# Transposing DMA of f by rows of four tokens (2 KB), with a sigmoid that puts the tokens back in order

## The chip, the cores and the metric

One core of a Trainium2 chip; the batches of runs fell on different chips, and every ratio is taken within a batch. The metric is the time of one execution in device microseconds (us). A run is called fast or slow: slow when it is more than 1.5% above the fastest run of the same kernel. Only fast runs are compared.

Engines: PE is TensorE (matmuls), PEld its weight loads, ACT is ScalarE, DVE is VectorE, POOL is GpSimd, SP is SyncE, whose queue (SPq) issues most DMAs here.

## The reference

A gated recurrence over 6,144 tokens of 4 sequences, 256 wide, feeds a two-layer feed-forward block:

```python
sig = 1.0 / (1.0 + np.exp(-f_logit))
f = lower_bound + (1.0 - lower_bound) * sig
h = f[:, t] * h + (1.0 - f[:, t]) * x[:, t]        # y[:, t] = h, over all t
h1, h2 = y @ w1, y @ w2                            # 256 -> 1024
out = np.maximum(h1, h2) @ w_out                   # 1024 -> 256
```

The kernel computes max(h1, h2) as h1 + relu(h2 - h1), so the first layer is one product with wd = w2 - w1, and h1 goes into the second layer through a precomputed 256 x 256 matrix. With u = sigmoid(-f_logit) the decay is 1 - (1 - lower_bound) u and the drive u x; the factor 1 - lower_bound is folded into the weights.

## The kernel before

The work goes in 48 blocks of 512 tokens. The recurrence needs the tokens along the free dimension and d on the partitions. The first 2,048 tokens are turned on TensorE; from then on (22 chunks of 1,024 tokens, 44 blocks) a GpSimd DMA casts f and x to bf16 into a DRAM scratch, and a transposing DMA on the SP queue brings them into SBUF turned:

```python
    def cross(c):
        nt = chunks[c][2]
        for s in range(2):                      # s = 0 is f, s = 1 is x
            if by_xbar(c, s):
                dst = inpool.tile([P, KC, CH], BF16, name=("fT", "xT")[s])
                nc.sync.dma_start_transpose(
                    out=dst[:, :, 0:nt], in_=held[c, s][0:nt, :]
                )
                held[c, s] = dst
```

The sigmoid of a block, and VectorE's five steps after it:

```python
    def gate(j):
        nb = blocks[j][2]
        u = midpool.tile([P, KC, TB], BF16, name="u")
        fT = turned[j, 0]
        nc.scalar.activation(
            out=like(u[:, :, 0:nb], fT), in_=fT, func=AF.Sigmoid, scale=-1.0
        )
        us[j] = u
    # scan_steps(j): decay(0), decay(1), drive (u * x), scan(0), scan(1)  -> y
```

The first layer of a block writes eight PSUM tiles dT, which ScalarE evicts with a relu, in the same queue as the sigmoids:

```python
    def first_layer(j, fc):
        # ... two matmuls of 512 columns into dT (pool ps_d, 3 buffers)
        nc.scalar.activation(out=rt[:, 0:nb], in_=dT[:, 0:nb], func=AF.Relu)
```

The main loop interleaves, for each of eight slots of block j, one first_layer of j and an eighth of the second layer of j - 1 (five matmuls of 256 columns), and puts the sigmoid of block j + 1 behind the eviction of slot 0:

```python
            for fc in range(FC):
                if j < NBLK:
                    first_layer(j, fc)
                if j > 2:
                    second_layer(j - 1, fc)
                # ... (turns on TensorE, first blocks only)
                if fc in gates:
                    gate(gates[fc])             # slot 0 for transposed chunks
                if fc == 0 and 2 < j < NBLK - 1:
                    scans = scan_steps(j + 1)
                if fc < len(scans):
                    scans[fc]()
```

## Time and profile before

| | before |
|---|---|
| timed runs | 400.79 us median of 3 (400.66 to 400.88) |
| profiled execution | 430.05 us, span 428.3 us, state slow |

The profile page, with the span, each engine's busy time, then TensorE and its granted clock in 40 slices of the span (busy tenths), then the chain of work that ended last:

```profile
span 428.3 us, 6970 instructions
...
PE 392.8 (92%) x2744; PEld 296.8 (69%) x2792; DVE 248.7 (58%) x359; ACT 268.5 (63%) x447; POOL 26.4 (6%) x58
...
PE   3999979798789999998997899999998999999996
...
PEclk9999999999989999999999699999999999999999
...
PE 46%; DMA 34%; SPq 15%; ACT 3%; DVE 1%; issue 1%; ACTq 0%
```

TensorE has holes between the sixth slice and the thirty-first, and a third of the chain is DMA. The windows of the same trace show two neighbouring blocks where nothing disturbs it, and one stretch where something does. The columns are the stretch, its length, then busy time and instructions of PE, PEld, DVE, ACT and POOL, the granted clock, the DMA share and GB/s:

```profile
323.63:331.45 7.82, 7.77 (x55) 5.96 (x56) 5.29 (x8) 5.50 (x10) 0.00 (x0) 1.00 1.21 195
331.45:339.27 7.82, 7.77 (x55) 5.95 (x56) 4.73 (x8) 5.49 (x9) 0.97 (x2) 1.00 1.02 220
110.00:120.00 10.00, 5.97 (x41) 4.26 (x40) 2.41 (x6) 4.01 (x8) 0.72 (x2) 0.98 0.99 152
```

A block takes 7.82 us when TensorE is fed. The instructions on the tile fT, the transposed f (duration min/median/max), and the DMAs' time from issue to landing:

```profile
L190 ACT ACTIVATE u<-fT x44: 1048/1051/1146, 41.2 to 405.5; 128x1024 bf16<-128x1024 bf16 x44
...
DMA to landing us min/median/max: 7.2/15.8/22.4
```

The sigmoid takes 1.05 us; f takes 15.8 us to land in this execution. A second look at the same kernel (b0_look), taken after the prediction, caught the fast state: it is a single run, to which the record gives no state, but at 400.91 us and a granted clock of 0.999 it lies with the fast ones. It is the one to compare with. Page, then the instructions on fT:

```profile
span 399.0 us, 7018 instructions
...
PE 388.5 (97%) x2792; PEld 295.0 (74%) x2792; DVE 249.1 (62%) x359; ACT 269.7 (68%) x447; POOL 26.3 (7%) x58
...
PE   3999999999999999999999999999999999999996
...
PE 97%; DMA 2%; SPq 1%; issue 0%; DVE 0%
```

### The profile page before, as it was taken

To read this page: it belongs to the slowest core of one execution; us is meant where nothing else is said; L and a number is where in the kernel's file an instruction comes from. 1 tells how busy PE (TensorE), PEld (TensorE's weight loads), DVE (VectorE), ACT (ScalarE), POOL (GpSimd) and SP (SyncE) were. 2 spreads that over 40 slices of the span, in tenths; PEclk is the share of its full clock that TensorE was granted. 3 is DMA by queue.
4 is the path that set the end of the run, shared out by engine and by line. 5 is a ranking of instruction groups with operands and counts; after the bars stand their busy time and mean duration, and the time that the engine had idled before them with its cause. 6 is when DMAs were issued, how large, how long until landed. Compare 5 with 4: busy or idle time off the path is not lost.

```text
span 428.3 us, 6970 instructions
## 1 busy us (share of the span) xinstructions
PE 392.8 (92%) x2744; PEld 296.8 (69%) x2792; DVE 248.7 (58%) x359; ACT 268.5 (63%) x447; POOL 26.4 (6%) x58
## 2 busy tenths in 40 slices
PE   3999979798789999998997899999998999999996
PEld 1677756576557777776775577767676777777775
DVE  5785637455357566564653557657547656567551
ACT  3656656557366676675673666756657676776762
POOL 1400000000000000000000000000000000000000
PEclk9999999999989999999999699999999999999999
DMA  7999999999999999999998999999999999998112
GB/s 245 222 220 198 123 157 141 137 169 252 81 240 226 119 239 233 112 248 168 183 237 75 218 158 186 250 145 170 219 131 231 226 216 164 268 157 179 79 69 100
DMA packets 103377, 77.01 MB, mean 180 GB/s; under 512 B 93552, under 2 KB 94064, under 8 KB 102640
## 3 DMA queue, kind: packets, MB, share of 16 engines
q1 hardware_dynamic: 100512, 51.13, 66.7%
q0 software_dynamic: 2544, 25.17, 36.1%
q8 instruction: 22, 0.36, 0.4%
q10 hardware_dynamic: 288, 0.26, 0.2%
q14 instruction: 11, 0.09, 0.1%
HBM read 53.48 MB, written 48.23 MB: 237 GB/s over the span
## 4 chain that ended last, share of the span: by engine, by line
PE 46%; DMA 34%; SPq 15%; ACT 3%; DVE 1%; issue 1%; ACTq 0%
PE psO L410 25%; DMA fT<-scr_0_90 20%; PE dT L381 19%; SPq L153 13%; DMA fT<-scr_1_91 12%; ACT u L190 2%; DMA w1n_110<-in_moe_w_dram 2%; SPq L433 1%; PE psO L352 1%; ACT rt L389 1%; PE tT L180 1%; PE psO L365 0%; SPq L121 0%; DVE osb L430 0%; DVE y L233 0%
## 5 line engine op out<-in xcount | busy, mean ns | idle before, releaser
L389 ACT ACTIVATE rt<-dT 128x512 bf16<-128x512 f32 x384 | 219.2, 598 | 104.1 <-PE dT L381 100.0
L381 PE MATMUL dT<-y,wd 128*128 128x512 bf16 x720 | 219.5, 384 | 21.3 <-ACT rt L389 19.5
L410 PE MATMUL psO<-wob,rt 128*128 128x256 bf16 x1536 | 230.7, 274 | 2.7 <-issue 0.4
L410 PEld LDWEIGHTS <-rt 128*128 128x128 bf16 x1536 | 170.7, 114 | 41.4 <-issue 1.1
L233 DVE TENSOR_TENSOR_SCAN y<-ff,y,v 128x512 bf16<-128x512 bf16 x88 | 107.9, 1268 | 0.1
L430 DVE COPY osb<-psO 128x512 f32<-128x512 f32 x94 | 64.7, 690 | 59.0 <-PE psO L410 58.9
L381 PEld LDWEIGHTS <-wd 128*128 128x128 bf16 x768 | 75.8, 99 | 33.2 <-issue 24.6
L209 DVE TENSOR_SCALAR ff<-u,nom 128x512 bf16<-128x512 bf16 x94 | 29.0, 351 | 105.0 <-ACT u L190 105.0
L410 PE MATMUL psO<-w_109,y 128*128 128x256 bf16 x384 | 74.0, 275 | 0.0
L410 PEld LDWEIGHTS <-y 128*128 128x128 bf16 x384 | 43.4, 113 | 42.6 <-issue 3.5
L190 ACT ACTIVATE u<-fT 128x1024 bf16<-128x1024 bf16 x44 | 46.4, 1054 | 35.5 <-DMA fT<-scr_1_91 18.2
L220 DVE TENSOR_TENSOR v<-u,xT 128x1024 bf16<-128x1024 bf16 x44 | 30.3, 688 | 3.8 <-DMA xT<-scr_0_92 1.8
L98 POOL DMA_DIRECT2D scr_0_90<-in_f_logit_dram x11 | 5.4, 493 | 149.7 <-DMA fT<-scr_0_90 149.7
L98 POOL DMA_DIRECT2D scr_1_91<-in_f_logit_dram x11 | 5.3, 486 | 148.8 <-DMA fT<-scr_1_91 148.1
L233 DVE TENSOR_TENSOR_SCAN y<-ff,v 128x512 bf16<-128x512 bf16 x6 | 7.0, 1208 | 0.0
L98 POOL DMA_DIRECT2D scr_0_92<-in_x_dram x11 | 5.4, 488 | 18.7 <-DMA xT<-scr_0_92 16.9
L98 POOL DMA_DIRECT2D scr_1_93<-in_x_dram x11 | 5.3, 486 | 15.7 <-DMA xT<-scr_1_93 14.9
L190 ACT ACTIVATE u<-tT 128x1024 bf16<-128x1024 bf16 x3 | 3.2, 1058 | 4.3 <-PE tT L180 4.3
L352 PE MATMUL psO<-ident_f,w1n_110 128*128 128x128 f32 x8 | 1.9, 422 | 3.4 <-DMA w1n_110<-in_moe_w_dram 3.4
L341 ACT ACTIVATE wd<-wdf,om 128x128 bf16<-128x128 f32 (+1 forms) x6 | 2.2, 428 | 4.3 <-DVE wdf L333 4.3
L352 PEld LDWEIGHTS psO<-ident_f,w1n_110 128*128 128x128 f32 x8 | 1.6, 221 | 3.7 <-issue 3.7
L220 DVE TENSOR_TENSOR v<-u,tT 128x1024 bf16<-128x1024 bf16 x3 | 3.6, 1216 | 0.0
(49 smaller groups left out, 45.1 us busy)
## 6 DMA issues: line engine op xcount, KB each, us to landing
out_dram<-osb SPq DMA_DIRECT2D x47, 512.0 KB, 4.8
scr_0_90<-in_f_logit_dram POOLq DMA_DIRECT2D x11, 512.0 KB, 7.5
scr_0_92<-in_x_dram POOLq DMA_DIRECT2D x11, 512.0 KB, 12.4
scr_1_91<-in_f_logit_dram POOLq DMA_DIRECT2D x11, 512.0 KB, 7.9
scr_1_93<-in_x_dram POOLq DMA_DIRECT2D x11, 512.0 KB, 13.6
fn<-in_f_logit_dram POOLq DMA_DIRECT2D x3, 256.0 KB, 7.9
xn<-in_x_dram POOLq DMA_DIRECT2D x3, 256.0 KB, 8.6
w2n_112<-in_moe_w_dram SPq DMA_DIRECT2D x1, 512.0 KB, 6.5
```

The lines of the kernel that those rows point to most:

```text
L98: nc.gpsimd.dma_start(out=scr[0:nt, :].rearrange("(p i) d -> p (i d)", p=P), in_=src.rearrange("(p i) d -> p (i d)", p=P),)
L153: nc.sync.dma_start_transpose(out=dst[:, :, 0:nt], in_=held[c, s][0:nt, :])
L180: nc.tensor.transpose(dst, src, ident[:])
L190: nc.scalar.activation(out=like(u[:, :, 0:nb], fT), in_=fT, func=AF.Sigmoid, scale=-1.0)
L209: nc.vector.tensor_scalar(out=ff[:, h, 0:nb], in0=u[:, h, 0:nb], scalar1=nom[:, h : h + 1], scalar2=1.0, op0=ALU.mult, op1=ALU.add,)
L220: nc.vector.tensor_tensor(out=like(v[:, :, 0:nb], xT), in0=like(u[:, :, 0:nb], xT), in1=xT, op=ALU.mult,)
L233: nc.vector.tensor_tensor_scan(out=y[:, h, 0:nb], data0=ff[:, h, 0:nb], data1=v[:, h, 0:nb], initial=init, op0=ALU.mult, op1=ALU.add,)
L352: nc.tensor.transpose(pt[:, kc, q, :], half(w1n, g)[:, kc, 2 * r + q], ident_f[:])
L381: nc.tensor.matmul(dT[:, 0:nb], lhsT=wd[:, kc, fc * P : (fc + 1) * P], rhs=y[:, kc, 0:nb], start=(kc == 0), stop=(kc == KC - 1),)
L389: nc.scalar.activation(out=rt[:, 0:nb], in_=dT[:, 0:nb], func=AF.Relu)
L410: nc.tensor.matmul(ps[:, r, :], lhsT=left, rhs=right, start=(s == 0 and (r == 0 or j == NBLK - 1)), stop=(s == n - 1 and (r == 1 or j == N ...
L430: nc.vector.tensor_copy(out=osb[:, 2 * g : 2 * g + 2, :], in_=ps[:])
```

## The change

The intent: the transposing DMA of f should read long rows. The 1,024 x 256 scratch is seen as 256 rows of 4 tokens (2 KB) in place of 1,024 rows of one (512 B). The result has f sorted by the position i of the token in its row: all tokens 0, 4, 8, ..., then 1, 5, 9, .... The sigmoid has to pass over all of f anyway, so it puts the tokens back: it reads runs of one i (128 neighbouring elements) and writes u with a step of 4 elements. x stays as it was, so that VectorE's multiply keeps its contiguous operands.

```diff
@@ cross
+                if wide_rows[s]:                      # (True, False): f only; RT = 4
+                    dst = inpool.tile([P, RT, KC, CH // RT], BF16, name=("fT", "xT")[s])
+                    nc.sync.dma_start_transpose(
+                        out=dst[:].rearrange("p i k r -> p (i k) r"),
+                        in_=held[c, s][0:nt, :].rearrange("(r i) d -> r (i d)", i=RT),
+                    )
+                    held[c, s] = dst[:].rearrange("p i k r -> p k r i")
+                else:
                     # ... as before
@@ gate
-        nc.scalar.activation(
-            out=like(u[:, :, 0:nb], fT), in_=fT, func=AF.Sigmoid, scale=-1.0
-        )
+        out = like(u[:, :, 0:nb], fT)
+        if by_xbar(blocks[j][3], 0):
+            out, fT = by_row(out), by_row(fT)
+        nc.scalar.activation(out=out, in_=fT, func=AF.Sigmoid, scale=-1.0)
@@
+    def by_row(t):
+        return t if len(t.shape) == 3 else t.rearrange("p k m i -> p k i m")
```

More of the change, by code (lines that the diff above doesn't have):

```diff
@@ L80 @@
     NSCR = 2
+    RT = 4
+    wide_rows = (True, False)
     scratch = [
@@ L151, in cross @@
             if by_xbar(c, s):
-                dst = inpool.tile([P, KC, CH], BF16, name=("fT", "xT")[s])
-                nc.sync.dma_start_transpose(
-                    out=dst[:, :, 0:nt], in_=held[c, s][0:nt, :]
-                )
-                held[c, s] = dst
+                if wide_rows[s]:
[6 more added lines that the diff above has]
+                else:
+                    dst = inpool.tile([P, KC, CH], BF16, name=("fT", "xT")[s])
+                    nc.sync.dma_start_transpose(
+                        out=dst[:, :, 0:nt], in_=held[c, s][0:nt, :]
+                    )
+                    held[c, s] = dst
     def turn_steps(j):
@@ L162, in turn_steps @@
             if by_xbar(c, s):
-                turned[j, s] = held[c, s][:, :, o : o + nb]
+                if wide_rows[s]:
+                    turned[j, s] = held[c, s][:, :, o // RT : (o + nb) // RT, :]
+                else:
+                    turned[j, s] = held[c, s][:, :, o : o + nb]
                 continue
@@ L189, in gate @@
         fT = turned[j, 0]
-        nc.scalar.activation(
-            out=like(u[:, :, 0:nb], fT), in_=fT, func=AF.Sigmoid, scale=-1.0
-        )
+        out = like(u[:, :, 0:nb], fT)
+        if by_xbar(blocks[j][3], 0):
+            out, fT = by_row(out), by_row(fT)
+        nc.scalar.activation(out=out, in_=fT, func=AF.Sigmoid, scale=-1.0)
         us[j] = u
@@ L197, in like @@
             return t
-        return t.rearrange("p k (m i) -> p k m i", m=P)
+        return t.rearrange("p k (m i) -> p k m i", m=src.shape[2])
+    def by_row(t):
+        return t if len(t.shape) == 3 else t.rearrange("p k m i -> p k i m")
     def scan_steps(j):
@@ L219, in drive @@
             xT = turned[j, 1]
+            operands = [like(v[:, :, 0:nb], xT), like(u[:, :, 0:nb], xT), xT]
+            if by_xbar(c, 1):
+                operands = [by_row(t) for t in operands]
             nc.vector.tensor_tensor(
-                out=like(v[:, :, 0:nb], xT),
-                in0=like(u[:, :, 0:nb], xT),
-                in1=xT,
-                op=ALU.mult,
+                out=operands[0], in0=operands[1], in1=operands[2], op=ALU.mult
             )
```

## The prediction

> **What bounds it now.** TensorE. From 323.6 to 339.3 us the windows show it busy 7.77 of every 7.82 us, one 512-token block each. Before about 32 us come block 0, the weights and block 1's first layer; after it 47 second and 46 first layers, 46.7 block times, about 365 us; then 4 us of tail. That sums to 401 us, plus 1.8 us between the profiled span (428.3) and its measured time (430.05). The timed runs take 400.79, so by this estimate they hardly stall. The profiled execution is 27 us longer: the windows show about 22 us of TensorE holes between 50 and 330 us, and the granted clock (mean 0.986, 0.78 at 230 us) explains about 6. The holes are waits for f: the chain of waits has 32% in f's transposes and 13% in the SP queue's issue of transposes. I take them for a property of the profiled execution, which must also record 103,377 DMA packets. On that reading the prediction hangs.
>
> **Why f is late there.** An f transpose takes a median 15.8 us from issue to landing, x's 9.3. The packet records show all 90,112 transposing packets at 256 B, median 18 ns, mean 35: 677 of them take over 1.28 us and make up 77 of 198 us per engine. They stand behind the casting DRAM-to-DRAM loads, whose 32 KB pieces take 2.5 us or more on the same engines. Undisturbed, x's transpose moves in 2.0 to 2.5 us (128 packets an engine at 18 ns). f's time is mostly company, not row length.
>
> **What the change does.** 22 transposes read 256 rows of 2 KB in place of 1,024 of 512 B. Bytes, loads, buffers, waits and instruction counts stay. The Trainium skill, "DMA: Bandwidth & Descriptors", section "SDMA does more than copy", gives the crossbar transpose as one of 256-byte tiles; this trace agrees (256 B packets although rows are 512 B). So I expect still 2,048 packets of 256 B per transpose, near 18 ns, and f's landing still set by the loads beside it. If the longer rows made longer packets, f would save at most 1 to 2 of its 2.3 us per chunk of 15.6 us of TensorE work. The danger is the opposite: 256 B read at a pitch of 2 KB might be slower.
>
> The sigmoid (44, mean 1,054 ns for 1,024 elements) will write 2-byte elements 8 bytes apart. The skill, "ScalarE: Activation LUTs", section "The pipeline for one element", says one element per cycle whatever the function; the sigmoid that reads PSUM with a stride takes 1,023 ns here, so strided reading is free. No strided write is in this trace; I expect 1.05 to 1.15 us. Even at 2.1 us ScalarE (busy 63%) has room: evictions take 0.6 us of a 0.98 us slot, and three PSUM buffers cover almost 2.9 us: an estimated 0 to 0.25 us for each of 44. VectorE sees the same layouts.
>
> **On the critical path:** nothing in the timed runs, or a microsecond. Predicted 400.4 us, range 397.5 to 405. Chances: faster by over 2% 0.03, within 2% 0.87, slower by over 2% 0.10.
>
> **What would show it.** Transposing packets still 90,112 of 256 B, median 18 ns; f's landing still 12 to 18 us; sigmoid 1.05 to 1.15 us; multiply 0.69 us unchanged; undisturbed blocks still 7.82 us. The profiled span may wander between 405 and 435 us without the timed runs following.
>
> **What would make it wrong.** Timed runs that do stall on f, and a transpose that gets much faster (then 396 at best: TensorE's floor stays). Reads at 2 KB pitch at twice 18 ns, or a sigmoid over 2 us holding up evictions (then 405 to 415).

## More of the kernel before

```profile
L190 ACT ACTIVATE u<-fT x44: 1050/1050/1146, 40.1 to 376.3; 128x1024 bf16<-128x1024 bf16 x44
...
DMA to landing us min/median/max: 4.7/6.1/15.7
```

Here TensorE is 97% of the chain, f lands after a median 6.1 us, and no engine waits for it.

## The result

| | before | changed |
|---|---|---|
| median | 400.84 us (4 runs, one of them slow, 409.82) | 412.18 us (4 runs, 411.48 to 412.30) |
| ratio of fast runs | | 1.0281, 95% interval 1.0261 to 1.0301 |
| sigmoid, 44 of them | 1.05 us | 2.50 us |
| block, start to start | 7.82 us | 8.07 us |
| f, issue to landing (median, fast state) | 6.1 us | 5.5 us |

A ratio here is the mean time of one kernel's fast runs over that of the other's fast runs of the same rounds, so it is not quite the ratio of the medians. The kernel became 2.8% slower. The profiled execution of the changed kernel was in the fast state. Its page, as above:

```profile
span 410.5 us, 6970 instructions
...
PE 392.4 (96%) x2744; PEld 294.9 (72%) x2792; DVE 245.4 (60%) x359; ACT 320.8 (78%) x447; POOL 27.0 (7%) x58
...
PE 57%; ACT 33%; issue 7%; DMA 2%; SPq 1%; ACTq 0%; DVE 0%
PE psO L427 29%; ACT u L206 27%; PE dT L398 25%; ACT rt L406 6%; DMA w1n<-in_moe_w_dram 2%; PE psO L369 1%; PE tT L193 1%; PE psO L382 0%; SPq L123 0%; ACTq L406 0%; SPq L465 0%; SPq L338 0%; DVE osb L436 0%
```

The chain now runs through ScalarE's sigmoid (L206) for 27% of the span; before, in the fast state, ScalarE was not in it. The instructions on fT:

```profile
L206 ACT ACTIVATE u<-fT x44: 2497/2500/2595, 40.6 to 387.6; 128x1024 bf16<-128x1024 bf16 x44
...
DMA to landing us min/median/max: 4.8/5.5/15.6
```

The hole is hard to see in the busy shares: TensorE reads 96% busy, and the page's group of first-layer matmuls waits for ScalarE for 0.2 us in all. The ends of matmuls are modelled, and a modelled end covers most of a hole of this size. Starts are better. The timeline of one block of the changed kernel, ScalarE first (start, us, then the instruction; neighbours are merged), then TensorE's first-layer matmuls with what lies between cut:

```profile
201.53 0.60 ACT L406 ACTIVATE rt<-dT 128x512 bf16<-128x512 f32 x1 [0.38 <-PE dT L398]
202.03 2.50 ACT L206 ACTIVATE u<-fT 128x1024 bf16<-128x1024 bf16 x1
204.27 2.14 ACT L406 ACTIVATE rt<-dT 128x512 bf16<-128x512 f32 x4
```

```profile
201.82 0.59 PE L398 MATMUL dT<-y,wd 128*128 128x512 bf16 x2
...
202.80 0.59 PE L398 MATMUL dT<-y,wd 128*128 128x512 bf16 x2
...
203.77 0.59 PE L398 MATMUL dT<-y,wd 128*128 128x512 bf16 x2
...
205.00 0.59 PE L398 MATMUL dT<-y,wd 128*128 128x512 bf16 x2
```

The slots start at 201.82, 202.80 and 203.77, 0.98 us apart. The fourth should start at 204.75 and starts at 205.00. It is the one that needs the PSUM buffer of the slot at 201.82, and that buffer's eviction stood behind the sigmoid: it began at 204.27, 2.24 us after the sigmoid did, and ended at 204.95, just before TensorE went on. (The profile lets an eviction begin shortly before the sigmoid ahead of it ends, here at 204.53.) From one such sigmoid to the next the trace has 8.07 us (202.03 to 210.10), 0.25 us more than 7.82. Times 44 blocks this is 11 us, against 11.3 us between the medians.

The same block of the kernel before, in the fast state; ScalarE holds no eviction for more than 0.95 us, and the slots behind the sigmoid keep their pace, 0.98 us apart:

```profile
204.30 1.05 ACT L190 ACTIVATE u<-fT 128x1024 bf16<-128x1024 bf16 x1
205.25 1.08 ACT L389 ACTIVATE rt<-dT 128x512 bf16<-128x512 f32 x2
206.68 0.60 ACT L389 ACTIVATE rt<-dT 128x512 bf16<-128x512 f32 x1 [0.35 <-PE dT L381]
```

```profile
204.09 0.59 PE L381 MATMUL dT<-y,wd 128*128 128x512 bf16 x2
...
205.07 0.60 PE L381 MATMUL dT<-y,wd 128*128 128x512 bf16 x2
...
206.05 0.59 PE L381 MATMUL dT<-y,wd 128*128 128x512 bf16 x2
...
207.03 0.59 PE L381 MATMUL dT<-y,wd 128*128 128x512 bf16 x2
```

### The profile page after: what moved, and what is told of

The parts are those of the page before. It is cut to its first block, busy times and chain, and to the rows that moved or that the text cites. A ratio compares the mean times of both kernels' runs of the same rounds, so it can differ in the third digit from the quotient of the medians.

```text
span 410.5 us, 6970 instructions
## 1 busy us (share of the span) xinstructions
PE 392.4 (96%) x2744; PEld 294.9 (72%) x2792; DVE 245.4 (60%) x359; ACT 320.8 (78%) x447; POOL 27.0 (7%) x58
## 4 chain that ended last, share of the span: by engine, by line
PE 57%; ACT 33%; issue 7%; DMA 2%; SPq 1%; ACTq 0%; DVE 0%
PE psO L427 29%; ACT u L206 27%; PE dT L398 25%; ACT rt L406 6%; DMA w1n<-in_moe_w_dram 2%; PE psO L369 1%; PE tT L193 1%; PE psO L382 0%; SPq L123 0%; ACTq L406 0%; SPq L465 0%; SPq L338 0%; DVE osb L436 0%
## 5 line engine op out<-in xcount | busy, mean ns | idle before, releaser
L406 ACT ACTIVATE rt<-dT 128x512 bf16<-128x512 f32 x384 | 216.5, 608 | 69.2 <-PE dT L398 68.3
L398 PE MATMUL dT<-y,wd 128*128 128x512 bf16 x720 | 216.8, 380 | 4.1 <-ACT rt L406 0.2
L206 ACT ACTIVATE u<-fT 128x1024 bf16<-128x1024 bf16 x44 | 110.1, 2502 | 0.0
L398 PEld LDWEIGHTS <-wd 128*128 128x128 bf16 x768 | 75.2, 98 | 21.9 <-issue 14.1
L427 PE MATMUL psO<-w,y 128*128 128x256 bf16 x384 | 73.2, 272 | 0.0
L100 POOL DMA_DIRECT2D scr<-in_f_logit_dram x22 | 10.8, 491 | 268.8 <-DMA fT<-scr 268.0
L100 POOL DMA_DIRECT2D scr<-in_x_dram x22 | 10.9, 494 | 34.5 <-DMA xT<-scr 32.3
L206 ACT ACTIVATE u<-tT 128x1024 bf16<-128x1024 bf16 x3 | 3.2, 1056 | 4.3 <-PE tT L193 4.3
L369 PE MATMUL psO<-ident_f,w1n 128*128 128x128 f32 x16 | 3.1, 352 | 3.4 <-DMA w1n<-in_moe_w_dram 3.4
L369 PEld LDWEIGHTS psO<-ident_f,w1n 128*128 128x128 f32 x16 | 2.7, 213 | 3.8 <-POOL waited L344 3.7
L143 PE MATMUL tT<-ident,nat 128*128 128x128 bf16 x16 | 2.4, 307 | 2.9 <-DVE nat L134 2.3
L350 DVE TENSOR_TENSOR wdf<-w2n,w1n 128x512 f32<-128x512 f32 (+1 forms) x5 | 4.4, 905 | 0.7 <-DMA w1n<-in_moe_w_dram 0.7
```

The lines of the kernel that those rows point to most:

```text
L100: nc.gpsimd.dma_start(out=scr[0:nt, :].rearrange("(p i) d -> p (i d)", p=P), in_=src.rearrange("(p i) d -> p (i d)", p=P),)
L206: nc.scalar.activation(out=out, in_=fT, func=AF.Sigmoid, scale=-1.0)
L350: nc.vector.tensor_tensor(out=wdf[:, :, cols].rearrange("p kc (q m) -> p kc q m", q=n), in0=half(w2n, g)[:, :, qs], in1=half(w1n, g)[:, :, ...
L369: nc.tensor.transpose(pt[:, kc, q, :], half(w1n, g)[:, kc, 2 * r + q], ident_f[:])
L398: nc.tensor.matmul(dT[:, 0:nb], lhsT=wd[:, kc, fc * P : (fc + 1) * P], rhs=y[:, kc, 0:nb], start=(kc == 0), stop=(kc == KC - 1),)
L427: nc.tensor.matmul(ps[:, r, :], lhsT=left, rhs=right, start=(s == 0 and (r == 0 or j == NBLK - 1)), stop=(s == n - 1 and (r == 1 or j == N ...
```

## The experiments

The theory: the strided write makes the sigmoid 1.45 us longer; that holds up the evictions for longer than three PSUM buffers can cover, and the excess is TensorE's hole. Rivals: the wide rows or the new timing of the transfers cost the time; the extra ScalarE time costs in proportion, threshold or not. In the batch of e1 to e3 five of the eight runs of the kernel before were slow, and the record's verdict on these three is "unclear"; read here are the ratios of the fast runs with their intervals. "Held" below is the time from the start of a sigmoid to the start of the next eviction.

### Is it the write or the rows? A two by two

**e1_wide_inorder**: wide rows kept, the sigmoid writes u in order and therefore reads f with a step.

```diff
         out = like(u[:, :, 0:nb], fT)
-        if by_xbar(blocks[j][3], 0):
-            out, fT = by_row(out), by_row(fT)
         nc.scalar.activation(out=out, in_=fT, func=AF.Sigmoid, scale=-1.0)
```

> Wide rows for f kept, the sigmoid writes u in order again and reads f with a step of 256 elements. Theory A (the loss is the strided write of the sigmoid, 2.50 us against 1.05, which holds up the evictions): sigmoid back to about 1.05 us, block period back to 7.82 us, time 400 to 402 us. Rival B (the wide rows or the changed timing of the transfers cost the time): stays at 410 to 412 us with a sigmoid of 1.05 us. Rival C (any strided access of SBUF by ScalarE is slow, reads as well): sigmoid about 2.5 us and time about 412 us. Beside it: if wide rows make the transposes robust, f's landing stays near 5.5 us and the profiled span is within 2 us of the timed runs; if not, the profile falls back to f landing in about 16 us and a span near 428 us.

Measured: correct, 401.42 us median (four runs, one slow at 424.2), ratio 1.0011 (0.9971 to 1.0052). The loss is gone with the rows still wide, so rival B falls. Two details missed. The sigmoid is not back to 1.05 us but takes 1.99: a read with a long step is slow as well, only less, and it stays free because it is short enough. And the profiled execution was a slow one (422.3 us, f landing in 14.5 us), so wide rows do not keep the kernel out of that state.

**e2_narrow_strided**: rows of one token as before, with the strided write alone (tokens permuted inside a block, wrong).

```diff
+        out = like(u[:, :, 0:nb], fT)
+        if by_xbar(blocks[j][3], 0):
+            out = out.rearrange("p k (m i) -> p k i m", i=4)
+            fT = fT.rearrange("p k (i m) -> p k i m", i=4)
+        nc.scalar.activation(out=out, in_=fT, func=AF.Sigmoid, scale=-1.0)
```

> Narrow rows as before, the sigmoid reads runs of 128 and writes with a step of 4 elements (tokens permuted inside a block: the result is wrong on purpose). Theory A: sigmoid 2.50 us, 8.07 us per block, 411 to 413 us, as with the wide rows. Rival B (wide rows cost it): 400 to 402 us. Also: is f's landing near 5.5 us here too (then the slower pace of TensorE, not the longer rows, quietens the transfers) or near 16 us (then the longer rows do)?

Measured: 412.11 us median (four runs, 411.49 to 412.27), ratio 1.0282 (1.0258 to 1.0307), sigmoid 2.50 us. The strided write alone gives the whole loss. f's landing, 5.6 us with narrow rows, is that of the changed kernel with wide ones, 5.5.

**b0_look**: the kernel before, unchanged, for a profile in the fast state.

> The kernel before, once more, for its profile. If its long profiled span (428 us, f landing in 16 us) is a property of being profiled, it comes again near 428 us; if it is a state that this kernel falls into at times, profiled or not (one timed run beside the changed kernel took 409.8 us), this look may show 399 to 401 us with f landing in 5 to 8 us.

Measured: 400.91 us, span 399.0 us, f landing in 6.1 us; its lines stand above. The 428 us of the first profile was a state, not the price of being profiled.

What the wide rows did to the transfers can now be read from the packet records, in fast profiles alone. "f, first to last packet" is the median of the last 15 of the 22 transposes of f, which mostly have no load beside them:

| kernel | row | packets of 256 B | ns per packet, median (mean) | f, first to last packet, us |
|---|---|---|---|---|
| b0_look | 512 B | 90,112 | 18 (22.9) | 2.2 |
| e2_narrow_strided | 512 B | 90,112 | 18 (22.2) | 2.0 |
| changed | 2 KB, f only | 90,112 | 18 (23.2) | 2.1 |
| e7_rows_1k (below) | 1 KB, f only | 90,112 | 18 (23.7) | 2.3 |
| e8_rows_4k (below) | 4 KB, f only | 90,112 | 18 (21.9) | 2.3 |

The row length changes nothing in these five profiles: the packets are of 256 bytes at 18 ns whatever the row, and the two kernels with 512 B rows differ as much in the last column as the others.

### Is it a threshold, and where?

**e3_dose2**: the kernel before with each of the 44 sigmoids issued twice in a row, in order, the second into a spare tile (**e6_dose3** below: three times).

```diff
+        for _ in range(1 if by_xbar(blocks[j][3], 0) else 0):   # 2 in e6_dose3
+            nc.scalar.activation(out=again[:, :, 0:nb], in_=fT, func=AF.Sigmoid, scale=-1.0)
         us[j] = u
```

> The kernel before with each of the 44 sigmoids issued twice in a row, the second into a spare tile; every access in order, so no stride at all. ScalarE is then held for about 2.0 us without an eviction, 0.95 us more than before. Threshold theory (only what goes beyond the cover of three PSUM buffers, about 2.25 us, reaches TensorE): 400 to 402 us. Rival (each extra us on ScalarE costs in proportion, 11.3 us for 44 x 1.45): about 407 to 408 us.

Measured: 401.18 us median (400.67 to 407.43, one slow), ratio 1.0006 (0.9963 to 1.0049). Evictions are held for 1.90 us, 0.95 more than before, at no cost. ScalarE's busy share rises to 76%, that of the slower changed kernel being 78%.

> The kernel before with each of the 44 sigmoids issued three times in a row, in order, the last two into a spare tile: ScalarE is held for about 2.9 us without an eviction. Threshold theory with a cover of about 2.25 us: a hole of about 0.65 us in each of 44 blocks, 29 us, so about 429 us (425 to 433). Proportional rival (11.3 us for 44 x 1.45 us): 2 x 0.92 us x 44 would cost about 14 us, 415 us.

Measured: 437.95 us median (five runs, 437.71 to 441.29), ratio 1.0924 (1.0905 to 1.0944). The evictions are held for 2.99 us and the blocks take 8.66 us, a hole of 0.84 us; times 44 this is 37 us. The threshold stands, and 415 us (proportion) is out. But the size was put too low, 29 us, because the cover was put too high. Here the profile names the eviction as what ended TensorE's wait:

```profile
202.70 0.59 PE L384 MATMUL dT<-y,wd 128*128 128x512 bf16 x2 [0.68 <-ACT rt L392]
```

A buffer comes free when its eviction ends, not when it begins. So count from the start of the (first) sigmoid to the end of the first eviction behind it, each time the median of the 44:

| kernel | held, us | to the end of that eviction, us | hole per block, us | difference of the last two, us |
|---|---|---|---|---|
| e3_dose2 | 1.90 | 2.48 | 0 | |
| changed | 2.24 | 2.92 | 0.25 | 2.67 |
| e6_dose3 | 2.99 | 3.57 | 0.84 | 2.73 |
| e8_rows_4k (below) | 4.27 | 5.19 | 2.52 | 2.67 |

The cover is about 2.7 us to the end of the eviction. This is the time between two uses of a buffer, 3 x 0.98 us, less the time from the first matmul of the slot to the start of the sigmoid (201.82 to 202.03 in the trace above). As holding it is no fixed number (2.0, 2.15 and 1.75 us in these three, not 2.25), as the eviction behind the sigmoid takes 0.69 us in the changed kernel and 0.93 in e8, in place of 0.59.

### Is it the holding of evictions, or ScalarE's load?

**e4_split_sigmoid**: the changed kernel, with the strided sigmoid cut into two, one for each half of d, the second behind the next eviction (the edit is shortened here).

```diff
+    def gate_half(j, h):
+        if h == 0:
+            us[j] = midpool.tile([P, KC, TB], BF16, name="u")
+        nc.scalar.activation(
+            out=us[j][:, h, :].rearrange("p (m i) -> p i m", i=RT),
+            in_=turned[j, 0][:, h].rearrange("p m i -> p i m"),
+            func=AF.Sigmoid, scale=-1.0,
+        )
@@ main loop
-                if fc in gates:
+                if fc == 0 and 0 in gates:
+                    gate_half(gates[0], 0)
+                elif fc == 1 and 0 in gates:
+                    gate_half(gates[0], 1)
+                elif fc in gates:
                     gate(gates[fc])
```

> The changed kernel with each of the 44 sigmoids cut into two (one for each half of d, same wide rows, same strided writes), the second behind the next eviction. ScalarE does the same slow work, even some 0.2 us more per block, but never goes more than about 1.3 us without an eviction. If the loss is the blocking of evictions beyond the cover of three PSUM buffers: 400 to 402 us, with ScalarE's busy time still near 320 us. If it is ScalarE's load: 412 us or more.

Measured: 408.36 us median (four runs, 408.09 to 408.46), ratio 1.0184 (1.0168 to 1.0200). A miss: only a third of the loss came back (what is left is under 2%, but it is clear of the noise). The evictions are no longer late; another wait took their place. VectorE first, then TensorE's matmuls of the last slot of one block and the first slot of the next:

```profile
202.93 0.35 DVE L238 TENSOR_SCALAR ff<-u,nom 128x512 bf16<-128x512 bf16 x1 [1.31 <-ACT u L204]
203.20 0.68 DVE L252 TENSOR_TENSOR v<-u,xT 128x1024 bf16<-128x1024 bf16 x1
203.80 0.68 DVE L459 COPY osb<-psO 128x512 f32<-128x512 f32 x1
204.40 2.33 DVE L262 TENSOR_TENSOR_SCAN y<-ff,v 128x512 bf16<-128x512 bf16 x2
```

```profile
205.54 0.59 PE L410 MATMUL dT<-y,wd 128*128 128x512 bf16 x2
...
206.52 0.64 PE L410 MATMUL dT<-y,wd 128*128 128x512 bf16 x2
```

The second half of u comes at 202.9 us, and multiply, a copy and both scans stand behind it; the scans end at 206.73. The matmul pair at 206.52 is the first to read that y, and its second matmul, which needs the second half of y, starts late (the pair takes 0.64 us in place of 0.59; 0.75 in the next block). From sigmoid to sigmoid that trace has 7.87 and then 7.97 us; over all its blocks the mean is 7.99, and 0.17 us more than 7.82, times 44, is 7.3 of the 7.5 us that stayed.

**e10_split_chain**: e4 with VectorE's steps cut at the same place.

```diff
+        def drive_half(h): ...                  # multiply of one half of d
+        def second_half():
+            scan(0); decay(1); drive_half(1)
+        if by_xbar(c, 0) and j >= 4:
+            return [decay(0), drive_half(0), second_half, scan(1)]   # (lambdas written short)
```

> e4_split_sigmoid once more, with VectorE's work on the block cut at the same place: decay, multiply and scan of the first half of d go before those of the second, so that VectorE no longer stands with all of it behind the second half of the sigmoid. In e4 the evictions were no longer held up, yet 7.5 us of the 11.3 stayed; in its trace the second scan ends just as TensorE wants y for the next block (206.52 to 206.73 us). If that late y is what stayed: y about 1 us earlier and 400 to 402 us, with ScalarE still at 318 us. If ScalarE's load or something else is: 408 us again.

Measured: correct, 401.14 us in the one fast run of four, which is also the profiled one; the others were slow (427.9 to 447.7), so there is no interval. In the profile of the fast run ScalarE is busy 319.0 us as in e4 (318.7), the blocks take 7.82 us, and y's second scan ends at 202.5 us, 1.0 us before TensorE starts on the next block at 203.48:

```profile
201.27 1.22 DVE L270 TENSOR_TENSOR_SCAN y<-ff,v 128x512 bf16<-128x512 bf16 x1
```

```profile
203.48 0.59 PE L430 MATMUL dT<-y,wd 128*128 128x512 bf16 x2
```

That is what a late y predicts, and ScalarE's load is excluded by this one run; a verdict from several runs is lacking.

**e5_four_dT** and **e11_four_dT_again**: the changed kernel with a fourth buffer for dT. So that no more of PSUM is used, psO gives one up. **e5_control** is the kernel before with the same buffers.

```diff
-        tc.tile_pool(name="ps_d", bufs=3, space=bass.MemoryType.PSUM)
+        tc.tile_pool(name="ps_d", bufs=4, space=bass.MemoryType.PSUM)
-        tc.tile_pool(name="ps_o", bufs=3, space=bass.MemoryType.PSUM)
+        tc.tile_pool(name="ps_o", bufs=2, space=bass.MemoryType.PSUM)
```

> The changed kernel with four PSUM buffers for dT in place of three (and two for psO in place of three). The cover grows by one slot of 0.98 us, so the 0.25 us hole in each block should close: 400 to 402 us, sigmoid still 2.50 us. If two psO buffers cost something by themselves, its control shows that. If the loss were elsewhere: 412 us.

Measured: 400.78 us in the one fast run; the other three were slow (408 to 435 us).

> The kernel before with the same four and two buffers. Theory: 400 to 402 us, no different from before, as nothing there waits for a dT or a psO buffer for long. If psO with two buffers is short, slower, and e5_four_dT has to be read against this.

Measured: ratio of the fast runs 0.9989 (0.9968 to 1.0011); two fast runs of four, both 400.52 us. Two psO buffers cost nothing that these runs show.

> e5_four_dT once more, as only one of its four runs was fast (400.78 us; the others, at lower granted clocks, 408 to 435). Theory: its fast runs are 400 to 402 us, against 412 for the changed kernel with three buffers; a profile in the fast state would show no hole in TensorE with a sigmoid of 2.50 us. If the fast run was an accident: 408 us or more in all.

Measured: 400.58 us median (six runs, one slow at 436.6), ratio 0.9998 (0.9984 to 1.0012). With the sigmoid as slow as ever the loss is gone. Sigmoid and block in the profile of this kernel, fast state:

```profile
L206 ACT ACTIVATE u<-fT x44: 2503/2504/2602, 39.7 to 375.9; 128x1024 bf16<-128x1024 bf16 x44
```

```profile
203.00:210.82 7.82, 7.77 (x57) 5.96 (x57) 4.88 (x8) 6.67 (x10) 0.49 (x1) 1.00 1.02 210
```

ScalarE works 6.67 of 7.82 us in this block and TensorE does not notice. This settles it for the changed kernel: its strided sigmoid costs time only by holding evictions beyond what the buffers cover.

### What does a strided write cost?

**e7_rows_1k** and **e8_rows_4k**: the whole change with rows of 2 and of 8 tokens (RT = 2, RT = 8), so writes with a step of 4 and of 16 bytes.

> The whole change with rows of 2 tokens (1 KB): the sigmoid reads runs of 256 and writes with a step of 2 elements (4 bytes). If any step other than one costs the same: sigmoid 2.5 us, 412 us. If the cost grows with the step: 1.4 to 2.0 us, under the threshold of 2.25 us, and 400 to 402 us. Transposes: still 90,112 packets of 256 B, 18 ns each, about 2.0 us undisturbed.

Measured: sigmoid 1.35 us; 401.58 us median (400.79 to 401.99), ratio 1.0010 (0.9987 to 1.0032). Slower by a third than in order (1.05), below the threshold, and free.

> The whole change with rows of 8 tokens (4 KB): the sigmoid reads runs of 64 and writes with a step of 8 elements (16 bytes). If any step other than one costs the same: 2.5 us and 412 us. If the cost grows with the step: 3.5 to 5 us, and by the threshold theory a hole of the excess over 2.25 us in each of 44 blocks, 55 us or more, over 455 us. Transposes as ever: 90,112 packets of 256 B, 18 ns, about 2.0 us undisturbed.

Measured: sigmoid 4.77 us; 517.14 us median (514.92 to 518.31), ratio 1.2886 (1.2844 to 1.2929). The blocks are 10.34 us apart in the trace, a hole of 2.52 us; times 44 this is 111 of the 116 us, and the granted clock of 0.99 accounts for some of the rest: in the trace two blocks that fall into stretches at half the clock take 12.02 us.

**e9_stride_bench**: sigmoids of 1,024 elements alone on ScalarE, and nothing else (its output is zeros).

> Not the kernel: four sigmoids each of 1,024 elements per partition alone on ScalarE, for several steps of reads and of writes, in 2-byte and 4-byte types (its output is zeros, wrong on purpose; only durations are read). In order about 1.05 us; write step 4 in 2-byte about 2.5 us as in the changed kernel; read step 256 about 1.98 us as in e1_wide_inorder; reads of PSUM with a step about 1.03 us. Open: step 2 and 8, 4-byte writes, runs of 2 and 4 elements. If the cost is a narrow write of 2 bytes, 4-byte elements with a step cost about 1.05 us; if it is the step as such, they cost about 2.5 us too. A write of 512 elements with step 4 should take near half: if the cost is per element, 1.3 to 1.4 us.

Measured, as groups of instructions (tile written <- tile read, shapes, count | busy us, mean ns). In the names wr is a write and rd a read with a step of c = 2, e = 4, i = 8 elements; bf and fp are 2-byte and 4-byte elements of the tile written; wrrunc and wrrune write runs of 2 and 4 elements, each followed by a gap of three times its length:

```profile
L73 ACT ACTIVATE wribf<-src 128x1024 bf16<-128x1024 bf16 x4 | 19.1, 4774 | 0.0
L73 ACT ACTIVATE wrebf<-src 128x1024 bf16<-128x1024 bf16 x4 | 10.7, 2674 | 0.0
L73 ACT ACTIVATE rdibf<-wide 128x1024 bf16<-128x1024 bf16 x4 | 7.9, 1983 | 0.0
L73 ACT ACTIVATE wrefp<-src 128x1024 f32<-128x1024 bf16 x4 | 7.9, 1975 | 0.0
L73 ACT ACTIVATE wrcbf<-src 128x1024 bf16<-128x1024 bf16 x4 | 5.4, 1338 | 0.0
L73 ACT ACTIVATE wrhalf<-src 128x512 bf16<-128x512 bf16 x4 | 5.3, 1321 | 0.0
L73 ACT ACTIVATE wrcfp<-src 128x1024 f32<-128x1024 bf16 x4 | 4.7, 1174 | 0.0
L73 ACT ACTIVATE wrrunc<-src 128x1024 bf16<-128x1024 bf16 x4 | 4.4, 1097 | 0.0
L73 ACT ACTIVATE rdebf<-wide 128x1024 bf16<-128x1024 bf16 x4 | 4.4, 1089 | 0.0
L73 ACT ACTIVATE dst<-src 128x1024 bf16<-128x1024 bf16 x4 | 4.1, 1034 | 0.0
```

In order it is 1,034 ns. A 2-byte write with a step costs 1,338 ns at 4 bytes, 2,674 at 8 and 4,774 at 16, so each element gets dearer the farther apart they are; the half-length one (1,321) shows that it goes by elements. The type matters as well as the distance, and neither of the two outcomes written down came out: 4-byte elements take 1,174 ns at 8 bytes, where 2-byte elements take 2,674, and 1,975 at 16 bytes, where 2-byte elements take 4,774. Pairs of 2-byte elements, 16 bytes from pair to pair, take 1,097, but these are 512 places to write and not 1,024. For each place 16 bytes from the last that is 4.7 ns for a single 2-byte element, 1.9 for a 4-byte element and 2.1 for a pair. So whatever fills a 4-byte word is cheaper than a single 2-byte element, and it too gets dearer at 16 bytes. That the chip handles the half-filled word differently is a reading of these numbers, not something they show. Reads hardly mind a step of 8 bytes (1,089) and nearly double at 16 (1,983). The bench is near the kernels but not equal to them: 2,674 ns against 2,500 at the step of the changed kernel, for which no run gives the reason.

## Why the prediction was wrong

- **Wrong: "No strided write is in this trace; I expect 1.05 to 1.15 us."** The sigmoid took 2.50 us. This is the step that failed. It rested on a strided read (of PSUM, 1.02 us) and on the Trainium skill's page "ScalarE: Activation LUTs", which gives one element per cycle for every function (the prediction names "The pipeline for one element"; the sentence stands a few lines on, under "Step-by-step: what each stage is for"). Neither says anything of writes. The prediction's "so strided reading is free" is no rule either: a read of SBUF with a long step took 1.99 us in e1. e2_narrow_strided gives the whole loss by the strided write alone; e1_wide_inorder takes it away by writing in order, at the price of that slower read.
- **Right in kind, short in size: "Even at 2.1 us ScalarE has room ... three PSUM buffers cover almost 2.9 us: an estimated 0 to 0.25 us for each of 44."** It is a threshold, as said: doubling the sigmoid's time is free (e3_dose2), a fourth buffer makes 2.50 us free (e11_four_dT_again), and at 2.50 us the price is the estimate's upper end, 0.25 us a block. The cover is about 2.7 us and not 2.9, and the eviction behind the sigmoid, 0.6 to 0.7 us, has to end within it. The estimate was made for a sigmoid of 2.1 us, where little or nothing would be lost (1.99 us was free in e1), so that its upper end fits a sigmoid of 2.50 us is partly luck. The prediction put the consequence of a sigmoid over 2 us at 405 to 415 us, and it was 412; it gave that only a chance of 0.10.
- **Right: the packets.** 90,112 of 256 B, median 18 ns, before and after, and with rows of 1 and 4 KB too. So in the fast state the rows brought nothing. In the slow profile of e1, with wide rows, the packets are the same and f still lands late (14.5 us). The skill's page "DMA: Bandwidth & Descriptors", section "SDMA does more than copy", describes the transpose by 256-byte tiles; all these traces agree.
- **Right: the timed runs hardly stall on f, and TensorE is the floor.** In the fast state TensorE is 97% of the chain at 7.82 us a block (b0_look).
- **Wrong, without consequence: the long profile as "a property of the profiled execution".** The second look was 399.0 us in its profile, and timed runs of the kernel before ran from 400.4 to 445.8 us. It is a state. The predicted landing of f, "still 12 to 18 us", was read off that state: it is 5.5 us in the fast profile of the changed kernel, but 6.1 in the fast one of before, so this is no gain.

No version beat the kernel before. The best of them (e1, e7, e11) equal it within 0.3%, as TensorE, 97% of the chain, leaves next to nothing to win there.

## What to carry to other kernels

When a layout change is to be "put back for free" by an instruction that passes over the data anyway, price the strided side of that instruction by itself before building the rest; here a small bench of the durations would have told about 2.5 us (it gave 2.67) from 1.05. Where one queue both evicts PSUM and does other work, the longest stretch without an eviction counts, not the busy share: what lies between its start and the end of the first eviction after it has to fit into the time between two uses of a buffer. A hole of a quarter of a microsecond can hide behind modelled matmul ends, so compare start to start.

## What the Trainium skill lacked or had wrong

- "ScalarE: Activation LUTs" (sections "Step-by-step: what each stage is for" and "What ACT_TABLE_LOAD costs") gives one element per cycle, with no word on strides in SBUF. Measured for 1,024 2-byte elements: 1,034 ns in order; written with a step of 2, 4 and 8 elements 1,338, 2,674 and 4,774 ns; read with a step of 4, 8 and of 256 elements 1,089, 1,983 and 1,904 ns; 4-byte elements written with a step of 2 and 4 elements 1,174 and 1,975 ns.
- "SBUF — State Buffer" (section "Door 1: The DMA port swizzle", note on 16-byte cachelines) lets one stride for free up to 8 bf16, if at least two accesses hit a line. For ScalarE's reads the two hits are right (1,089 ns at a step of 4), but a step of 8 already takes 1,983 ns. For its writes of 2-byte elements the note does not hold: two hits a line cost 2,674 ns, four hits 1,338. The note's limit of 4 elements for fp32 does not hold for its writes either (1,975 ns). For ScalarE in SBUF no page tells strided reads from writes, or 2-byte from 4-byte writes.
- "DMA: Bandwidth & Descriptors" (section "DMA Transpose (X-bar)") does not say whether the length of the source row matters. Here it does not, from 512 B to 4 KB: 2,048 packets of 256 B a transpose, median 18 ns, 2.0 to 2.3 us from the first packet to the last.
- No page that was read describes the slow state. Of the kernel before, 11 of 37 timed runs were slow, at 409.8 to 445.8 us, and in its slow profile f took 15.8 us to land in place of 6.1. Kernels with a hole in every block (the changed one, e2, e4, e6, e8) had none in 21 runs; of the changed versions without holes e10 and e5 had three of four, e1 one of four, e11 one of six and e7 none of four. Why is open, and nothing above rests on it.
